# Multi-query attention with a parallel FFN on one core: the FFN's input weights load behind the q weights, the other weights behind the first q tile

## The chip, the core and the metric

One core of a Trainium2 chip runs the whole kernel in one launch. The metric is device microseconds of an execution. Before the change the median of six runs is 739.34 us (738.37 to 739.84).

TensorE (PE) multiplies, ScalarE (ACT) does exponentials and tanh, VectorE (DVE) and GpSimd (POOL) do elementwise work, and SyncE (SP) issues nearly all transfers. Each engine takes its instructions strictly in the order in which the program lists them, and waits on semaphores where data come from another engine or from a transfer.

## What is computed

```python
xn = _layernorm(x, axis=-1)                 # x: 1 x 2048 x 640
q = (xn @ wq)  # 32 heads of 20;  k = xn @ wk, v = xn @ wv: one head of 20 for all
scores = jnp.einsum("bhqd,bkd->bhqk", q, k) * (Dh ** -0.5)
p = _softmax(scores, axis=-1)
o = jnp.einsum("bhqk,bkd->bhqd", p, v)
A = o.transpose(0, 2, 1, 3).reshape(B, S, H * Dh) @ wo
B = silu(xn @ w1) @ w2                      # 640 -> 1728 -> 640
return x + A + B
```

All inputs and the output are bfloat16. There is one batch of 2048 rows.

## The kernel before

**Tiles and steps.** The 2048 rows are four chunks of 512 queries (QC) and 16 key tiles of 128 (KT). A unit is one head of one chunk, 128 in all; three units make a group, and a group takes 16 steps, one for each key tile. A step (`do_S`, L750) is up to three 128x512 score tiles, one for each unit, in three PSUM banks (L769). The 43 groups make 688 steps; the last group has two units. The exponential of a step is one ACT instruction over two or three tiles (L787). Where `want_dve` (L740) says so, the third tile goes to DVE instead: it is clipped into an integer that is read as a bfloat16 (L801), and two shifted copies of it, one from DVE (L869, up to three tiles at once) and one from POOL (L807), are added up with it by PE. PV (L857) are the products with v; a tile on DVE needs three or more of them. They come in four column groups of one bank, which DVE evacuates at the end of a group (L972), a transposing transfer turns (L931) and POOL normalizes (L939 to L958).

**The other work.** The FFN of a chunk is 14 first products of five matmuls (`h_job`, L1084), each with a tanh on ACT (L1092, into one of the two halves of `tb`) and a multiply on DVE (L1097), and then eight half tiles of 14 matmuls each (`out_job`, L1146; 448 in all). The output projection is L1151, 144 in all; in the last chunk some of it is held in PSUM (L1209, L1214). The q tiles of a chunk are `qd_job` (L1050): DVE evacuates one (L1057), and SP copies its heads to their rows in `qT` (L1066), five to eight transfers each. The first eight heads of chunk 0 come from two q jobs of their own (`q_job`, L1025).

**What sets the order.** Nothing is ordered by the hardware's timing: `Sched` plays the program through before it is built, with a guessed duration for each operation, and writes down one list for each engine. PE asks `step` (L565): a score row if it can run, else PV, else a matmul of the next job in `misc`, else a filler matmul on zeros (L687, L693, L706). Jobs of `misc` come strictly in turn and mostly share one PSUM bank (7). `fill_chunk` (L1227) puts a chunk's jobs in when its first score row comes, each with a step before which it may not begin (L1256 to L1265). On other engines the ready operation with the lowest priority number is next; an operation with `lock` set is planned apart from the locked ones of the other of DVE and POOL.

**The prologue.** `prologue` (L1284) loads x in 16 row tiles, takes means and variances (DVE L1411 and L1413, or ACT L1396 and L1399 for ACT_STATS), and an inverse root by two Newton rounds for each batch of BATCHES on the engine in NW_ENG (`newton`, L1440: nine small operations on DVE, twelve on POOL). It normalizes (`norm`, L1429, the engine in NORM_ENG: L1436 on POOL or DVE, L1431 on ACT) and transposes, on PE (`tr_job`, L1511, evacuated at L1522) or with a transfer for the tiles in DT (L1489). Keys (`k_job`, L1532, evacuated at L1540, shifted copy on POOL at L1542), values (L1556, L1565) and q jobs follow in the order of PRO. SP's list is: four x, a part of wq, twelve x, the rest of wq (L1321), the transposes as they come, two fills of the unused rows of `qT` from `tb` (L1500), w1 (L1503), wo (L1505), four x tiles again (L1222), w2 (L1326), then the q copies. w2 lies over the normalized x tiles and waits for their transposes. POOL doubles wo (L1547) behind the last key job.

Of the kernel before, what the change touches and what calls it, by code (L numbers as in the profile page):

```python
# [12 lines left out]
ALU = mybir.AluOpType  # L13

P = 128
D = 640
H = 32
DH = 20
DC = 5
# [5 lines left out]
QC = S // QW  # L25
KT = S // P
F = 1728
FC = 14
FLAST = F - 13 * P
HT = 8  # L30
# [15 lines left out]
NBLK = 31  # L46
NZ = 4
ZB = 3
Y_POOL = True
Y_TIME = 0.72  # L50
Y_LOCK = False
Y_SLOW = 0.1
H_FIRST = 4
NEARLY = 2
LASTPV = 16
DVE_LAST = 1
ZWAIT = 6
SWITCH = 0.105
S_LEAD = 0.56
PV_PRESS = 12  # L60
DVE_TH = 2.8
U_PRIO = 1.1
X_PRIO = 0.8
PACE = (0.9, 0.9, 0.9, 0.9)
# [4 lines left out]
OVER = 0.1  # L69
FLUSH_G = 0  # L70
NOD = 0
PV_HOLD = 9
Q_EVERY = 2
DT_ISSUE = 1.28
UT_ISSUE = 1.05
DT = (4, 5, 8, 9, 10, 11, 12, 13, 14, 15)
NORM_P = 0.5
DVE_FROM = 8
PRO = "t6 v0 k2 t7 k3 k4 q1 v1 v2 k5 k6 k7 v3 d0"
ACT_STATS = (4, 6, 9, 12, 14)  # L80
NW_ENG = ("dve", "pool", "dve", "pool")
NORM_ENG = ("pool", "pool", "pool", "pool", "dve", "act", "act", "dve", "act", "dve", "dve", "act")
BATCHES = ((0, 4), (4, 8), (8, 12), (12, 16))


class Op:
# [268 lines left out]
class Builder:  # L355
# [382 lines left out]


    def want_dve(self, t):  # L740
        if t < DVE_FROM or t % KT >= KT - NOD or t >= self.T - DVE_LAST:
            return False
        sc = self.sc
        back = sc.t["dve"] - sc.t["pe"]
        for op in sc.pend["dve"]:
            back += op.dur
        back += len(self.zblocks) * 0.6
        return back < DVE_TH

    def do_S(self, t, now):  # L750
        sc = self.sc
# [1 line left out]
        us = self.groups[g]  # L753
        nh = len(us)
        self.started = True
        for c in sorted(set(x // H for x in us)):
            if c not in self.filled:
                self.filled.add(c)
                self.fill_chunk(c, t)
        dv = self.want_dve(t)  # L760
# [282 lines left out]
    def qd_job(self, c, m, step=-1):  # L1043
        sc = self.sc
        lo, hi = (Q0 if c == 0 else QN)[m]
        rows = hi - lo
        mms = []
        for k in range(DC):
            def f(pe, b, k=k):
                return pe.matmul(self.bk(b, 0, QW, 0, rows), self.wq[:, k, lo:hi], self.xnT[:, k, c * QW:(c + 1) * QW],  # L1050
                                 start=(k == 0), stop=(k == DC - 1))
            mms.append((t_mm(QW), f))

        def consume(b):
            sl = self.nqd % 2
            self.nqd += 1
            sc.new("dve", t_dve_ps(QW), lambda v: v.tensor_scalar(self.qd[0:rows, sl, :], self.bk(b, 0, QW, 0, rows), C1,  # L1057
                                                                  None, ALU.mult), [("B", b)], [("qd", sl)],
                   prio=X_PRIO, name=f"qev{c}_{m}")
            sem = sc.sem(f"q{c}_{m}")  # L1060
            ops = []
            heads = range(lo // DH, -(-hi // DH))
            for h in heads:
                a, z = max(lo, h * DH), min(hi, h * DH + DH)
                r = (h % 4) * SLOT + a - h * DH
                ops.append(sc.dma("sp", lambda q, a=a, z=z, r=r, h=h: q.dma_start(  # L1066
                    self.qT[r:r + z - a, h // 4, c % 2, :], self.qd[a - lo:z - lo, sl, :]), [("qd", sl)],
                    [("qb", c % 2, h)], (z - a) * QW * 2, sem=sem, name="qdma"))
# [158 lines left out]
    def fill_chunk(self, c, t):  # L1227
# [56 lines left out]
    def prologue(self):  # L1284
# [19 lines left out]
        def load_w(eng, key, pieces, tag, nb, over=()):  # L1304
            deps = sc.deps_of((), [tag] + list(over))
# [13 lines left out]
        for n in range(4, NT):  # L1319
            load_x(n)  # L1320
        load_w("sp", "q", [lambda q, c=c: q.dma_start(self.wq[:, c, 80:], self.A_wq[c * P:(c + 1) * P, 80:])  # L1321
                           for c in range(DC)], ("wqd", 1), P * D * 2)
        w2p = []
        for fk in range(FC):
            rows = P if fk < FC - 1 else FLAST
            w2p.append(lambda q, fk=fk, rows=rows: q.dma_start(self.w2[0:rows, fk, :],  # L1326
                                                               self.B_w2[fk * P:fk * P + rows, :]))

        def load_w2():
            load_w("sp", "2", w2p, ("w2",), P * D * 2, [("xn", i) for i in range(14)] + [("idf",)])  # L1330
# [98 lines left out]
        def norm(n, eng, prio, ra):  # L1429
            if eng == "act":  # L1430
                np_("act", t_act(D) + 0.186, lambda v: v.activation(  # L1431
                    xa(n), self.xslot(n), AF.Identity, scale=self.rstd[:, n:n + 1],
                    bias=self.nb[:, n:n + 1]), self.xkeys(n) + [("nb", n), ("rs", ra)], [("xn", n)],
                    prio=prio, name=f"norm{n}")
                return
            np_(eng, 0.36 if eng == "dve" else 0.87, lambda v: v.tensor_scalar(  # L1436
                xa(n), self.xslot(n), self.rstd[:, n:n + 1], self.nb[:, n:n + 1], ALU.mult, ALU.add),
                self.xkeys(n) + [("nb", n), ("rs", ra)], [("xn", n)], prio=prio, name=f"norm{n}")

        def newton(a, b_, pr, eng):  # L1440
            v_ = self.tmp[:, 0, a:b_]
# [3 lines left out]

            def nw(fn, r, w):
                ch.append(np_(eng, 0.09 if eng == "dve" else 0.16, fn, r, w, prio=pr, name="nw"))
                if len(ch) > 1:
                    ch[-2].then = ch[-1]
            nw(lambda v: v.tensor_scalar(v_, self.mv[:, a:b_, 1], EPS, None, ALU.add), mvk(a, b_), [("va", a)])  # L1450
# [43 lines left out]
        pool(0.95, lambda g: g.tensor_scalar(self.tb[:, 0, :], self.zero[:, 0:QW], self.offq[:, :], 1.0, ALU.add, ALU.mult),  # L1494
             [("zero",), ("offq",)], [("tb", 0)])
        tb = self.tb[:, 0, :]
        for par in range(2):
            h0 = 2 if par == 0 else 0
            rep = bass.AP(self.tb, tb.offset, [list(tb.ap[0]), [0, HT - h0], list(tb.ap[1])])
            op = sc.dma("sp", lambda q, par=par, h0=h0, rep=rep: q.dma_start(self.qT[:, h0:HT, par, :], rep), [("tb", 0)],  # L1500
                        [("qb", par, h) for h in range(4 * h0, H)], P * (HT - h0) * QW * 2, sem=sem(f"qz{par}"))
            op.inc_no = 1
        load_w("sp", "1", [lambda q, c=c: q.dma_start(self.w1[:, c, :], self.B_w1[c * P:(c + 1) * P, :])  # L1503
                           for c in range(DC)], ("w1",), P * F * 2)
        load_w("sp", "o", [lambda q, c=c: q.dma_start(self.wo[:, c, :], self.A_wo[c * P:(c + 1) * P, :])  # L1505
                           for c in range(DC)], ("wo",), P * D * 2)
        def tr_job(n):
            mms = []
            for k in range(DC):
# [5 lines left out]
            def consume(b):  # L1515
                src = self.bk16(b)[:, 0:DC * P].rearrange("p (c t) -> p c t", c=DC)
                dst = self.xnT[:, :, n * P:(n + 1) * P]
                if n in (0, 2):
                    sc.new("act", t_act(D), lambda a: a.activation(dst, src, AF.Copy), [("B", b)], [("xnT", n)],
                           prio=2.0, name=f"xT{n}")  # L1520
                else:
                    sc.new("dve", 0.40, lambda v: v.tensor_copy(dst, src), [("B", b)], [("xnT", n)],  # L1522
                           prio=0.5 if n < 4 else 3.0, name=f"xT{n}")
                if n == max(i for i in range(13) if i not in DT):
                    load_w2()
            return Job(f"tr{n}", mms, xnk(n)[:1] + [("idb",)], consume)

        def k_job(j):
# [7 lines left out]
            def consume(b):  # L1536
# [4 lines left out]
                       name=f"kev{j}")  # L1541
                sc.new("pool", t_pool(256), lambda g: g.tensor_scalar(d1, dst, self.offk[:, :], 1.0, ALU.add,  # L1542
                                                                      ALU.mult), [("kT", j), ("offk",)],
                       [("kT1", j)], prio=1.0, name=f"k1_{j}")
                if j == KT // 2 - 1:
                    for c in range(DC):
                        pool(0.7, lambda g, c=c: g.tensor_scalar(self.wo[:, c, :], self.wo[:, c, :], 2.0, 1.0, ALU.mult,  # L1547
                                                                 ALU.mult), [("wo",)], [("wo",)], prio=2.0)
# [100 lines left out]
```

## Time and profile before

| | |
|---|---|
| median of six runs | 739.34 us |
| profiled execution, its own time | 739.32 us |
| its span, first to last instruction | 737.5 us |
| PE busy (matmuls, ends modelled) | 710.8 us, 96% |
| ACT busy | 691.4 us, 94%, of it L787 658.3 in 688 |
| DVE busy | 665.7 us, 90%, of it L801 432.8 in 646 |
| POOL busy | 538.3 us, 73% |
| mean granted PE clock | 0.991 |
| first, last score row | 16.7 us, 710.6 us |
| first tanh (L1092) | 64.86 us, behind 32 exponentials |
| w1 issued by SP | 39.5 to 44.9 us |
| w2 issued by SP | 49.7 to 56.4 us |

Times are from the start of the span. In a row of the timeline the first number is the start, the second the time to the end of the last of the merged instructions; the bracket is how long the engine was idle before, and who ended that. The duration of an instruction is longer than the distance to the next one, because they overlap at their ends: what counts in a full engine is the distance from start to start.

### The profile page before, as it was taken

How to read it: one execution, taken by the hardware profiler on the slowest of the kernel's cores; microseconds unless marked ns; L12 is line 12 of the kernel's file. 1: busy time of each engine (PE TensorE's matmuls, PEld its weight loads, DVE VectorE, ACT ScalarE, POOL GpSimd, SP SyncE). 2: the span in 40 equal slices, each digit the busy share in tenths (PEclk: the TensorE clock that was granted, in tenths of full speed). 3: DMA queues.
4: the chain of work that ended last, by engine and by line, in shares of the span. 5: the costliest groups of instructions: out<-in, count | busy, mean ns of one | idle time of the engine just before them, and what ended most of it. 6: DMA issues, size and time to landing. Idle time of an engine off the chain costs nothing.

```text
span 737.5 us, 18883 instructions
## 1 busy us (share of the span) xinstructions
PE 710.8 (96%) x6798; PEld 229.9 (31%) x6852; DVE 665.7 (90%) x1206; ACT 691.4 (94%) x780; POOL 538.3 (73%) x929
## 2 busy tenths in 40 slices
PE   9799999999999999999999999999999999999998
PEld 4422222233332223223333322222233332322245
DVE  7778998999999999989999999999999999989973
ACT  6878999999999999999999999999999999999940
POOL 5458777787787777777878877777787877777750
PEclk9879999999999999999999999999999999999999
DMA  6494010000002021100001101110002000200101
GB/s 191 79 324 126 18 24 17 21 17 16 9 16 44 17 58 40 34 8 9 9 8 27 34 16 43 52 31 16 8 9 44 10 8 16 80 9 8 31 16 36
DMA packets 58466, 29.14 MB, mean 40 GB/s; under 512 B 44390, under 2 KB 57734, under 8 KB 58374
## 3 DMA queue, kind: packets, MB, share of 16 engines
q1 hardware_dynamic: 56918, 27.71, 14.7%
q8 instruction: 56, 0.92, 0.5%
q10 hardware_dynamic: 1456, 0.22, 0.2%
q14 instruction: 36, 0.29, 0.1%
HBM read 11.36 MB, written 2.62 MB: 19 GB/s over the span
## 4 chain that ended last, share of the span: by engine, by line
PE 61%; ACT 19%; DVE 5%; issue 5%; POOL 0%; DVEq 0%; ACTq 0%; POOLq 0%
PE psall L857 21%; PE psall L769 20%; ACT sbt L787 17%; PE psall L1146 9%; PE psall L1084 5%; DVE sbt L801 3%; PE psall L1151 2%; PE psall L1050 2%; ACT sbt L1092 2%; DVE sbt L869 1%; PE psall L693 0%; DVE sbt L972 0%; DVE sbt L1057 0%; PE psall L1214 0%; DVE sbt L1097 0%
## 5 line engine op out<-in xcount | busy, mean ns | idle before, releaser
L787 ACT ACTIVATE sbt<-psall 128x1024 bf16<-128x1024 f32 (+2 forms) x688 | 658.3, 1090 | 15.3 <-PE psall L769 14.4
L807 POOL TENSOR_TENSOR sbt<-sbt 128x256 int32<-128x256 int32 x646 | 447.2, 698 | 150.8 <-DVE sbt L801 122.4
L801 DVE TENSOR_SCALAR sbt<-psall 128x512 int16<-128x512 f32 x646 | 432.8, 684 | 34.8 <-PE psall L769 27.4
L769 PE MATMUL psall<-sbt 32*128 32x512 bf16 x2048 | 270.1, 386 | 7.9 <-ACT sbt L787 4.4
L857 PE MATMUL psall<-sbt 128*32 128x512 bf16 x3524 | 270.4, 385 | 2.1 <-DVE sbt L869 0.7
L769 PEld LDWEIGHTS psall<-sbt 32*128 32x128 bf16 x2048 | 68.6, 91 | 252.8 <-issue 103.0
L869 DVE TENSOR_SCALAR sbt<-sbt 128x1536 int16<-128x1536 int16 (+2 forms) x230 | 134.6, 586 | 2.8
L857 PEld LDWEIGHTS psall<-sbt 128*32 128x32 bf16 x3524 | 67.7, 94 | 113.1 <-issue 76.1
L1146 PE MATMUL psall<-sbt 128*128 128x320 bf16 x448 | 86.2, 302 | 0.0
L1084 PE MATMUL psall<-sbt 128*128 128x512 bf16 (+1 forms) x242 | 75.5, 384 | 5.0 <-issue 3.5
L1146 PEld LDWEIGHTS psall<-sbt 128*128 128x128 bf16 x448 | 35.1, 97 | 43.4 <-issue 33.8
L1097 DVE SCALAR_TENSOR_TENSOR sbt<-sbt,psall 128x512 bf16<-128x512 bf16 (+1 forms) x56 | 38.1, 680 | 4.3 <-ACT sbt L1092 3.7
L1092 ACT ACTIVATE sbt<-psall 128x512 bf16<-128x512 f32 (+1 forms) x56 | 37.8, 675 | 0.0
L972 DVE CAST sbt<-psall 128x512 bf16<-128x512 f32 x43 | 29.3, 682 | 2.5 <-PE psall L857 2.4
L1084 PEld LDWEIGHTS psall<-sbt 128*128 128x128 bf16 (+1 forms) x280 | 18.8, 98 | 39.2 <-issue 28.2
L1050 PE MATMUL psall<-sbt 128*128 128x512 bf16 (+1 forms) x81 | 26.6, 385 | 2.7 <-issue 1.4
L1151 PE MATMUL psall<-sbt 128*128 128x320 bf16 x144 | 28.7, 303 | 0.4 <-DVE sbt L1181 0.4
L944 POOL TENSOR_TENSOR sbt<-sbt 128x44 f32<-128x44 f32 x84 | 25.2, 300 | 1.0
L958 POOL TENSOR_TENSOR sbt<-sbt 128x240 bf16<-128x240 f32 (+2 forms) x44 | 25.5, 579 | 0.6 <-DVE sbt L949 0.2
L706 PE MATMUL psall<-sbt 128*128 128x512 bf16 (+2 forms) x67 | 18.1, 418 | 4.5 <-DVE sbt L1565 3.0
L1178 ACT ACTIVATE sbt<-psall 128x320 bf16<-128x320 f32 x4 | 1.5, 438 | 20.7 <-PE psall L1151 20.7
L942 POOL CAST sbt<-sbt 128x168 f32<-128x168 bf16 x42 | 14.1, 336 | 7.6 <-DMA sbt<-sbt 7.5
(94 smaller groups left out, 222.2 us busy)
## 6 DMA issues: line engine op xcount, KB each, us to landing
sbt<-in_A_x_dram SPq DMA_DIRECT2D x32, 160.0 KB, 3.5
out_dram<-sbt SPq DMA_DIRECT2D x15, 160.0 KB, 1.9
sbt<-in_B_w_dram SPq DMA_DIRECT2D x5, 432.0 KB, 7.3
sbt<-sbt SPq DMA_DIRECT2D x105, 20.0 KB
sbt<-in_B_w_dram SPq DMA_DIRECT2D x13, 160.0 KB, 5.7
sbt<-sbt SPq DMA_TRANSPOSE x68, 2.4
sbt<-sbt SPq DMA_DIRECT2D x1, 1024.0 KB, 7.3
sbt<-in_A_wo_dram SPq DMA_DIRECT2D x5, 160.0 KB, 6.8
```

Of the source, the lines that this page charges most:

```text
L769: ins = pe.matmul(self.bk(par3 + j), self.kT[r:r + SLOT, kk, kt * P:(kt + 1) * P], self.qT[r:r + SLOT, h // 4, (x // H) % 2, :], start=Tru ...
L787: return a.activation(self.E[:, b0 * QW:(b0 + na) * QW], self.ps[:, par3 * BANK:(par3 + na) * BANK], AF.Exp, scale=ACT_SCALE)
L801: return v.tensor_scalar(self.Z[:, zs, zp * QW:(zp + 1) * QW], self.bk(bb), 0.0, ZMAX, ALU.max, ALU.min)
L807: sc.new("pool", Y_TIME, lambda v: v.tensor_tensor(self.Y[:, zs, 1, zp * QW:(zp + 1) * QW].bitcast(I32), self.Z[:, zs, zp * QW:(zp + 1) * ...
L857: return pe.matmul(self.bk(UBANK, 0, QW, q * SLOT, (q + 1) * SLOT), self.v[:, w, kt, :], x, start=start, stop=stop, tile_position=(0, q * ...
L869: sc.new("dve", Y_SLOW + t_dve_4x(w), lambda v, k=k: v.tensor_scalar(self.Y[:, zs, k, 0:n * QW], Z, float(PH[k + 1][0]), None, ALU.add), z ...
L1050: return pe.matmul(self.bk(b, 0, QW, 0, rows), self.wq[:, k, lo:hi], self.xnT[:, k, c * QW:(c + 1) * QW], start=(k == 0), stop=(k == DC - 1))
L1084: return pe.matmul(self.bk(b, 0, QW, 0, rows), self.w1[:, k, fk * P:fk * P + rows], self.xnT[:, k, c * QW:(c + 1) * QW], start=(k == 0), s ...
L1092: sc.new("act", t_act(QW), lambda a: a.activation(t, src, AF.Tanh, scale=0.5), [("B", b)], [("tb", tp)], prio=X_PRIO, name=f"th{c}_{fk}")
L1097: sc.new("dve", t_dve_ps(QW), lambda v: v.scalar_tensor_tensor(out=self.hT[0:rows, fk, :], in0=t, scalar=1.0, in1=src, op0=ALU.add, op1=AL ...
L1146: return pe.matmul(self.bk(b, 0, 320), self.hT[0:rows, fk, i * P:(i + 1) * P], self.w2[0:rows, fk, e0:e0 + 320], start=(m == 0), stop=(m = ...
L1151: return pe.matmul(self.bk(b, 0, 320), self.oT[:, k, i * P:(i + 1) * P], self.wo[:, k, e0:e0 + 320], start=(m == 0 and src != "ps"), stop= ...
```

## The change

It has six parts.

1. w1 goes to SP right behind the rest of wq, ahead of the transposes.
2. w2, wo, the doubling of wo and the second fill of `qT` wait for the first q tile's evacuation (`late_loads`, called by `qd_job(0, 0)`); w2 used to be queued behind a transpose job, wo ahead of it.
3. A chunk's jobs are put in `misc` AHEAD = 30 steps before its first score row, with due steps as much earlier; in chunk 0 they may begin at step H0_STEP = 10 (16 before).
4. The inverse roots are taken in three batches of 4, 6 and 6 tiles, all on DVE; norms are shared out anew (ACT 6, POOL 5, DVE 5, the first four included); NORM_P is their priority; norms, Newton operations and the shifted key copies are locked between DVE and POOL.
5. The prologue's jobs stand in another order, with the q tile d0 behind v2 instead of last.
6. Constants of the planner: the share of DVE tiles (DVE_TH), the pressure at which PV goes first, the hold before the first PV, the first FFN jobs ahead of the projection, and when q jobs are mixed in (Q_FROM).

```diff
+AHEAD = 30
+Q_FROM = 8
+H0_STEP = 10
+KT_ACT = ()
-H_FIRST = 4
+H_FIRST = 8
-PV_PRESS = 12
-DVE_TH = 2.8
+PV_PRESS = 8
+DVE_TH = 2.6
-PV_HOLD = 9
+PV_HOLD = 11
-DT = (4, 5, 8, 9, 10, 11, 12, 13, 14, 15)
-NORM_P = 0.5
+DT = (4, 5, 6, 9, 10, 11, 12, 13, 14, 15)
+NORM_P = 4.5
-PRO = "t6 v0 k2 t7 k3 k4 q1 v1 v2 k5 k6 k7 v3 d0"
+PRO = "v0 t7 t8 v1 k2 k3 k4 q1 v2 d0 k5 k6 k7 v3"
-NW_ENG = ("dve", "pool", "dve", "pool")
-NORM_ENG = ("pool", "pool", "pool", "pool", "dve", "act", "act", "dve", "act", "dve", "dve", "act")
-BATCHES = ((0, 4), (4, 8), (8, 12), (12, 16))
+NW_ENG = ("dve", "dve", "dve")
+NORM_ENG = ("pool", "pool", "pool", "pool", "act", "pool", "act", "act", "dve", "act", "act", "act")
+BATCHES = ((0, 4), (4, 10), (10, 16))
...
-        for c in sorted(set(x // H for x in us)):
-            if c not in self.filled:
+        for c in range(QC):
+            if c not in self.filled and t >= self.first_step[c] - AHEAD:
...
+            if c == 0 and m == 0:
+                self.late_loads(("qd", sl))
...
-            if qs and n % Q_EVERY == Q_EVERY - 1:
+            if qs and n >= (Q_FROM if c else 0) and n % Q_EVERY == Q_EVERY - 1:
...
+        s0 -= AHEAD
+        s1 -= AHEAD
         if c == 0:
-            s0 += KT
+            s0 = H0_STEP
...
+        load_w("sp", "1", [lambda q, c=c: q.dma_start(self.w1[:, c, :], self.B_w1[c * P:(c + 1) * P, :])
+                           for c in range(DC)], ("w1",), P * F * 2)
...
-        for par in range(2):
+        def qz(par, extra=()):
...
+        qz(0)
+
+        def late_loads(key):
+            load_w2([key])
+            load_w("sp", "o", [lambda q, c=c: q.dma_start(self.wo[:, c, :], self.A_wo[c * P:(c + 1) * P, :])
+                               for c in range(DC)], ("wo",), P * D * 2, (), [key])
+            for c in range(DC):
+                pool(0.7, lambda g, c=c: g.tensor_scalar(self.wo[:, c, :], self.wo[:, c, :], 2.0, 1.0, ALU.mult, ALU.mult),
+                     [("wo",)], [("wo",)], prio=2.0)
+            qz(1, [key])
+        self.late_loads = late_loads
```

KT_ACT is empty and changes nothing. The norms', Newton's and key copies' `.lock = True`, and the lines that loaded w1, wo and w2 at their old places, are left out above.

More of the change, by code (lines that the diff above doesn't have):

```diff
@@ L740, in want_dve @@
     def want_dve(self, t):
-        if t < DVE_FROM or t % KT >= KT - NOD or t >= self.T - DVE_LAST:
+        if t < DVE_FROM or t % KT >= KT - NOD or t >= self.T - DVE_LAST or t % KT in KT_ACT:
             return False
@@ L1302, in load_x, with load_w @@
             op.inc_no = 1
-        def load_w(eng, key, pieces, tag, nb, over=()):
-            deps = sc.deps_of((), [tag] + list(over))
+        def load_w(eng, key, pieces, tag, nb, over=(), extra=()):
+            deps = sc.deps_of(extra, [tag] + list(over))
             for f in pieces:
@@ L1327, in prologue, with load_w2 @@
                                                                self.B_w2[fk * P:fk * P + rows, :]))
-        def load_w2():
-            load_w("sp", "2", w2p, ("w2",), P * D * 2, [("xn", i) for i in range(14)] + [("idf",)])
+        def load_w2(extra):
+            load_w("sp", "2", w2p, ("w2",), P * D * 2, [("xn", i) for i in range(14)] + [("idf",)], extra)
         np_ = sc.new
@@ L1437, in norm @@
                 xa(n), self.xslot(n), self.rstd[:, n:n + 1], self.nb[:, n:n + 1], ALU.mult, ALU.add),
-                self.xkeys(n) + [("nb", n), ("rs", ra)], [("xn", n)], prio=prio, name=f"norm{n}")
+                self.xkeys(n) + [("nb", n), ("rs", ra)], [("xn", n)], prio=prio, name=f"norm{n}").lock = True
         def newton(a, b_, pr, eng):
@@ L1447, in nw @@
                 ch.append(np_(eng, 0.09 if eng == "dve" else 0.16, fn, r, w, prio=pr, name="nw"))
+                ch[-1].lock = True
                 if len(ch) > 1:
@@ L1496, in prologue @@
         tb = self.tb[:, 0, :]
-        for par in range(2):
+        def qz(par, extra=()):
             h0 = 2 if par == 0 else 0
             rep = bass.AP(self.tb, tb.offset, [list(tb.ap[0]), [0, HT - h0], list(tb.ap[1])])
-            op = sc.dma("sp", lambda q, par=par, h0=h0, rep=rep: q.dma_start(self.qT[:, h0:HT, par, :], rep), [("tb", 0)],
+            op = sc.dma("sp", lambda q: q.dma_start(self.qT[:, h0:HT, par, :], rep), [("tb", 0)] + list(extra),
                         [("qb", par, h) for h in range(4 * h0, H)], P * (HT - h0) * QW * 2, sem=sem(f"qz{par}"))
             op.inc_no = 1
[L1503 to L1506, printed above, removed]
+        qz(0)
[8 more added lines that the diff above has]
+        self.late_loads = late_loads
         def tr_job(n):
@@ L1523, in consume @@
                            prio=0.5 if n < 4 else 3.0, name=f"xT{n}")
-                if n == max(i for i in range(13) if i not in DT):
-                    load_w2()
             return Job(f"tr{n}", mms, xnk(n)[:1] + [("idb",)], consume)
@@ L1543, in consume @@
                                                                       ALU.mult), [("kT", j), ("offk",)],
[L1544 to L1548, printed above, removed]
+                       [("kT1", j)], prio=1.0, name=f"k1_{j}").lock = True
             return Job(f"kv{j}", mms, [("xnT", 2 * j), ("xnT", 2 * j + 1), ("wk",), ("ost", 2, 0), ("ost", 2, 1)], consume)
```

## The prediction

> **What bounds the kernel now.** I read the page first, then the busy time by stage, then ScalarE's (ACT) and TensorE's (PE) instructions in order of time, then the waits.
>
> ```profile
> span 737.5 us, 18883 instructions
> ...
> ACT  6878999999999999999999999999999999999940
> ...
> PEclk9879999999999999999999999999999999999999
> ```
>
> ACT is full from the fifth slice to the last but two. It loses time at the start and at the end, and the granted PE clock dips only at the start. By stage (columns: PE, PEld, DVE, ACT, POOL busy us, then clock, DMA share, GB/s):
>
> ```profile
> 17.18:38.86 21.68, 17.48 (x152) 8.73 (x152) 16.24 (x52) 17.96 (x19) 11.21 (x29) 0.86 0.44 78
> 38.86:86.30 47.44, 44.28 (x406) 12.82 (x411) 39.05 (x71) 40.14 (x44) 34.26 (x56) 0.92 0.54 176
> 86.30:700.00 613.70, 599.64 (x5901) 183.77 (x5950) 577.41 (x996) 612.53 (x678) 472.76 (x789) 1.00 0.11 24
> 710.60:737.50 26.90, 23.46 (x180) 13.98 (x179) 10.01 (x25) 2.64 (x6) 1.83 (x3) 1.00 0.07 26
> ```
>
> A "step" is one row of score matmuls (L769) and its exponential (L787); there are 688. Step 8 starts its exponential at 38.86, step 50 at 86.3, and the last score row is at 710.6. So there are three regimes: a start with holes in ACT, 614 us in which ACT idles 1.2 us, and a tail of 26.9 us in which ACT does 2.64 us and PE works alone. The tail, PE by time:
>
> ```profile
> 711.96 1.90 PE L857 MATMUL psall<-sbt 128*32 128x512 bf16 x25
> 713.80 1.33 PE L1146 MATMUL psall<-sbt 128*128 128x320 bf16 x7
> 716.74 10.61 PE L1146 MATMUL psall<-sbt 128*128 128x320 bf16 x70
> 727.29 2.35 PE L1151 MATMUL psall<-sbt 128*128 128x320 bf16 x16
> 732.73 1.33 PE L1151 MATMUL psall<-sbt 128*128 128x320 bf16 x8
> ```
>
> L1146 is the FFN's second product. 10.61/70 = 0.152 us each, back to back: this backlog is the end of the kernel. Then ACT in order of time, with its idle time in brackets, and SP's issues:
>
> ```profile
> 29.55 1.45 ACT L787 ACTIVATE sbt<-psall 128x1536 bf16<-128x1536 f32 x1 [2.50 <-PE psall L769]
> 30.90 1.72 ACT L1431 ACTIVATE sbt<-sbt 128x640 bf16<-128x640 bf16 x2
> 38.86 1.02 ACT L787 ACTIVATE sbt<-psall 128x1024 bf16<-128x1024 f32 x1 [0.39 <-PE psall L769]
> 47.07 4.90 ACT L787 ACTIVATE sbt<-psall 128x1024 bf16<-128x1024 f32 x5 [2.84 <-PE psall L769]
> 67.84 1.94 ACT L787 ACTIVATE sbt<-psall 128x1024 bf16<-128x1024 f32 x2 [2.34 <-PE psall L769]
> 505.56 3.92 ACT L787 ACTIVATE sbt<-psall 128x1024 bf16<-128x1024 f32 x4
> 509.18 0.79 ACT L1092 ACTIVATE sbt<-psall 128x512 bf16<-128x512 f32 x1
> ```
>
> ```profile
> 49.70 6.70 SPq L1326 DMA_DIRECT2D sbt<-in_B_w_dram  x14
> 59.10 5.78 SPq L1066 DMA_DIRECT2D sbt<-sbt  x7
> ```
>
> Three large holes. At 29.55 PE waited for key and value evacuations behind a slow DVE. At 47.07 the last key job (its POOL copy is at 45.99) held the score row. At 67.84 step 32 is the first that needs heads 8 and on, whose seven q copies were issued only at 59.1 to 64.9, behind w2's fourteen pieces. ACT's pitch when full is (509.18 − 505.56)/4 = 0.905 us for two tiles; a third tile makes it about 1.35 (29.55 to 30.90), so 0.43 us a tile.
>
> **What the Trainium skill says.** "SBUF — State Buffer", Who interferes with whom: VectorE and GpSimd share one port pair under an exclusive lock, so tiny ops can be blocked for a neighbour's whole instruction. The trace agrees:
>
> ```profile
> 7.33 0.20 DVE L1451 TENSOR_SCALAR sbt<-sbt 128x4 int32<-128x4 int32 x1
> ...
> 19.92 0.83 DVE L1451 TENSOR_SCALAR sbt<-sbt 128x4 int32<-128x4 int32 x1
> ```
>
> The second ran beside POOL's norm (L1436). "TensorE: Matmul & The Clock Gate", What's actually happening: an idle window halves PE's clock; the trace has a clock of 0.86 before 38.86, where PE is idle 4.2 of 21.7 us. "DMA: Bandwidth & Descriptors", Queues, rings and completion order: SP's transfers are taken in ring order on each DMA engine, and a semaphore lands only after earlier writes. The trace agrees: x lands 3.5 us after issue (median), w1 and wo in the crowd at 39 to 47 us after 7.3 and 6.8.
>
> **The change part by part.** How instructions move I take from the order of the built programs, which holds no times; all durations are from the trace.
>
> *Tail.* After the last score row the old order has 89 L1146 matmuls, the new one 10: FFN chunks are opened AHEAD = 30 steps earlier. 79 × 0.152 = 12.0. The ten that stay still cover the waits for the last evacuation and its PE transposes (716.5, 5.9 after the last row). Check from the other end: 5.9, transposes 0.2, 8 matmuls of L1151 1.2, the 24 of L1209 and L1214 3.3 (729.34 to 732.60), 8 more 1.3, and 3.4 from PE's end to the span's end make 15.3 against 26.9. I take **−11.7**.
>
> *ACT's work.* The new order has 626 tiles on DVE instead of 646, so 20 tiles move to ACT: 20 × 0.43 = 8.6. Two more norms on ACT: 2 × 0.86 = 1.7 (row at 30.90). By place: before step 50 four tiles and two norms, less one tanh (0.48) that comes later, +2.9. From step 50 on 16 tiles and that tanh, **+7.3**; ACT has no idle time there to hide it. Relieved are DVE (20 × 0.68 of L801, some 17 us in all) and POOL (20 × 0.70), which bound nothing there.
>
> *PE's work in that phase.* It takes up the 79 matmuls (12.0) and 1.3 us of FFN and q matmuls that came before step 50, and loses some 37 PV matmuls at about 0.054 (12 take 0.22 more than 8), so about +11. The room is in the score rows' waits:
>
> ```profile
> PEld psall L769 <- ACT sbt L787: 63.2, 164, 0.7
> PEld psall L769 <- DVE sbt L801: 45.1, 112, 0.8
> ```
>
> Each begins 0.23 us after the row before anyhow (the "issue" rows), so the true waits are 63.2 − 164 × 0.23 = 25 and 45.1 − 112 × 0.23 = 19: 44 us. ACT's +7.3 widens it. Bounds of the extra cost: −4 (S no longer waits for DVE as often) to +4 (all 11 that isn't under ACT's 7.3). I take **+1.2**.
>
> *The start.* The gaps of ACT between 17.18 and step 50 are 0.82, 2.50, 0.39, 0.39, 0.51, 0.37, 2.84, 0.42, 0.31, 2.34: 10.9. In the new order: (a) both later inverse-root batches run on DVE, six tiles each, locked against POOL's norms; nine ops at about 0.2 make 2.0 us (7.12 to 9.13) instead of 4.1 (19.36 to 23.5), so norms 10 to 15 can start near 26.4 where ACT, after norm 8, two exponentials and the q weight copy, is free at 25.4: about 1.0 for 0.82. (b) Exponential 4 stands behind five norms, so the 2.50 is filled with work. (c) The holes of 0.3 to 0.5 lie under PE's half clock; I let all six (2.4) stay. (d) The last key job stands behind 11 score rows, not 14; 0.5 stays. (e) The first q tile (d0) moves ahead of the last keys: evacuated near 37, its copies leave behind the transposes (36.1), one fill and four x loads (2.6) and eight w2 pieces (3.8), by 43 to 48. Step 8 now comes near 37 (ACT free at 30.8 behind the norms, four wide exponentials at 1.35, some gap), step 32 at 37 + 24 × 0.905 + 2 × 0.43 + 1.5, near 61, so 2.34 goes. Left 3.9 of 10.9: −7.0, with +2.9 above **−4.1**. Bounds: −7.5 and +2.9.
>
> *What is moved in SP's queue.* w1 goes out at 11.2 to 16.5, where SP idles until 19.89; its data (2.2 MB at the 350 GB/s seen at 40 to 50 us, an estimate of 6.3) end about when the first transpose starts, so 0, at worst 1. w2, wo and the second fill go behind the first q evacuation: 14 pieces (6.7), seven copies (5.8), wo (2.5), fill: SP is through near 54 to 56. Two waits hang on this. The scaling of wo stands in POOL before about the 22nd third-tile add (L807): wo lands near 60, POOL is there near 60; behind it are those adds, and PE's PV rows behind them. And the first tanh writes tb, which the second fill reads: so although the first FFN matmuls stand at steps 18 and 19, the tanh stands behind 36 exponentials, near 66, and the fill lands at 59 to 63. I cost both at 0, with up to 3 us above. **FFN jobs don't really begin early**: at step 100 the new order has 55 first-product matmuls against 60. The gain in order comes over the next 500 steps.
>
> Sum: 737.5 − 11.7 + 7.3 + 1.2 − 4.1 = 730.2. The profiled execution took 739.32 with this span, 1.8 around it, and is at the median (739.34): **732.0**.
>
> **Rivals.** *Holes stay* (the start isn't filled as the order intends): +2.9 in place of −4.1, 739.0. For it: the wait near 67 only moves to other late loads. Against: the three big holes each lose their cause. *PE adds up with ACT*, the slower one: from step 50 on both are over 97% busy, and each score row waits for the later of PE and ACT; if waits no longer overlap, PE's 11.3 come on top of ACT's 7.3: 732.0 + 10.1 = 742.1. It decides as soon as it costs over 8.5 of those 11.3. For it: L1146 blocks of three or four must fit between score rows. Against: 44 us of waits, and ACT alone is late on almost every row. *DVE's relief counts*: −4 for +1.2, and the start at its best, −7.5: 732.0 − 5.2 − 3.4 = 723.4; at half of both 727.7.
>
> **How the numbers follow.** Forecast (728 to 737) 0.65; DVE's relief (723 to 728) 0.10; holes stay (737 to 740.5) 0.12; PE adds up (740.5 to 745) 0.13. The range 726 to 740 leaves out the slower case and about half of the better one. 0.2%, about what a measurement of this kernel can tell from no change, is 1.5 us: faster is below 737.9 (all of the first two, a sixth of the third, 0.77), same 0.10, slower 0.13.
>
> **What would show it.** PE after the last score row: ten L1146, about 15 us to the end; if it is 27 the order isn't what I read. ACT from step 50 to the last exponential: longer by 8.5; 15 or more is the slower rival. Step 50 at about 82 (before 86.3), no idle time over 1.5 before it. If ACT idles before its first tanh, or POOL before the wo scaling, the late loads bite.

## The result, and the profile after

The changed kernel takes 737.23 us in the median of 18 runs (735.45 to 739.49), the kernel before 739.51 in 37. The ratio is 0.9965 with an interval of 0.9957 to 0.9973: 0.3% faster, where 1.0% was forecast. The sign was right, the time is inside the range, and about two thirds of the gain is missing. The profiled execution took 737.44 us, with a span of 735.6.

From the page of the changed kernel, the span, ScalarE's (ACT's) busy tenths and the granted clock of TensorE (PE):

```profile
span 735.6 us, 18666 instructions
...
ACT  6996999999999999999999999999999999999972
...
PEclk9998999999999999999999999999999999999999
```

From the fifth slice on ACT is full up to the last two, which are a 7 and a 2 in place of 4 and 0. But its fourth slice (55 to 74 us) is only a 6, and the PE clock dips in that same slice. Busy time by stage, columns as before:

```profile
38.36:85.77 47.41, 41.23 (x399) 12.16 (x402) 34.84 (x63) 40.86 (x43) 31.75 (x52) 0.93 0.42 125
85.77:700.00 614.23, 599.69 (x5820) 187.11 (x5866) 560.54 (x961) 612.23 (x670) 451.55 (x759) 1.00 0.10 23
720.24:735.60 15.36, 11.29 (x98) 6.72 (x96) 7.34 (x18) 2.56 (x5) 2.58 (x4) 0.95 0.13 43
```

The last row is the tail from the last score row on: 15.4 us in place of 26.9. The first row is where the gain is missing: ACT is busy 40.86 of 47.41 us. PE at the start of the tail shows the ten matmuls of the FFN's second product that are left (L1152 here, L1146 before):

```profile
720.56 2.12 PE L861 MATMUL psall<-sbt 128*32 128x512 bf16 x28
722.62 1.12 PE L1152 MATMUL psall<-sbt 128*128 128x320 bf16 x7
...
723.69 0.67 PE L1152 MATMUL psall<-sbt 128*128 128x320 bf16 x3
```

ACT's rows with idle time ahead of them, up to step 50:

```profile
26.70 4.17 ACT L1441 ACTIVATE sbt<-sbt 128x640 bf16<-128x640 bf16 x5 [0.49 <-DVE sbt L1479]
...
39.88 22.47 ACT L791 ACTIVATE sbt<-psall 128x1024 bf16<-128x1024 f32 x23 [0.50 <-PE psall L861]
...
66.17 1.02 ACT L791 ACTIVATE sbt<-psall 128x1024 bf16<-128x1024 f32 x1 [3.81 <-PE psall L773]
...
68.63 1.02 ACT L791 ACTIVATE sbt<-psall 128x1024 bf16<-128x1024 f32 x1 [1.44 <-PE psall L773]
...
71.71 3.28 ACT L791 ACTIVATE sbt<-psall 128x1536 bf16<-128x1536 f32 x3 [0.55 <-PE psall L773]
```

The three large holes of before (2.50, 2.84, 2.34) are gone: after 39.88 ACT runs 23 exponentials without a gap. In their place a new hole of 3.81 + 1.44 + 0.55 = 5.80 us stands at steps 34 to 37. A score row (L773) is named as what ended it each time, so the question is what held that row. PE, then GpSimd (POOL), then the issues on SP, each in order of time:

```profile
60.35 0.39 PE L773 MATMUL psall<-sbt 32*128 32x512 bf16 x3
...
64.39 0.40 PE L861 MATMUL psall<-sbt 128*32 128x512 bf16 x4 [3.64 <-POOL sbt L811]
...
65.51 0.61 PE L773 MATMUL psall<-sbt 32*128 32x512 bf16 x3 [0.65 <-DVE sbt L805]
```

```profile
55.34 0.92 POOL L811 TENSOR_TENSOR sbt<-sbt 128x256 int32<-128x256 int32 x1 [0.55 <-DVE sbt L805]
62.34 0.33 POOL L946 CAST sbt<-sbt 128x168 f32<-128x168 bf16 x1 [6.08 <-DMA sbt<-sbt]
```

```profile
52.78 2.48 SPq L1519 DMA_DIRECT2D sbt<-in_A_wo_dram  x5
55.30 0.69 SPq L1512 DMA_DIRECT2D sbt<-sbt  x1
56.03 2.18 SPq L935 DMA_TRANSPOSE sbt<-sbt  x1
```

Read from the bottom. SP issues the transpose of group 0's U (L935) at 56.03, right behind wo and the second fill of qT (L1512, 1 MB). It lands 6.2 us after its issue; the median of the 42 transposes of this kind in the same profile is 2.4. POOL waits 6.08 us for it at L946, the first operation of group 0's normalisation. POOL's third-tile adds (L811) are queued behind, a PV row (L861) waits for one of those for 3.64 us, and the score row is queued behind the PV row on PE. The row that then comes takes 0.61 us in place of 0.39: PE has been idle, and the granted clock in the trace is 0.50 from 65.2 to 72.0. That is the larger part of the 1.44, but not of the 0.55: in the first kernel below, whose clock stays at 1.00, ACT waits 0.59 and 0.49 at the same two steps. The fall of the clock agrees with the Trainium skill, "TensorE: Matmul & The Clock Gate", What's actually happening, which says that a window of idleness halves the clock.

The trace of the kernel before already had this wait, only shorter. There the transpose (L931) goes out behind w2, lands after 5.0 us, and POOL waits 1.62 for it:

```profile
57.76 1.23 SPq L931 DMA_TRANSPOSE sbt<-sbt  x1
62.77 0.33 POOL L942 CAST sbt<-sbt 128x168 f32<-128x168 bf16 x1 [1.62 <-DMA sbt<-sbt]
```

### The profile page after: what moved, and what is told of

The parts are those of the page before. It is cut to its first block, busy times and chain, and to the rows that moved or that the text cites. A ratio compares the mean times of both kernels' runs of the same rounds, so it can differ in the third digit from the quotient of the medians.

```text
span 735.6 us, 18666 instructions
## 1 busy us (share of the span) xinstructions
PE 705.3 (96%) x6746; PEld 229.0 (31%) x6798; DVE 649.9 (88%) x1180; ACT 701.3 (95%) x782; POOL 517.1 (70%) x886
## 4 chain that ended last, share of the span: by engine, by line
PE 72%; ACT 13%; DVE 9%; issue 5%; DMA 0%; POOL 0%; DVEq 0%; ACTq 0%; POOLq 0%
PE psall L861 24%; PE psall L773 23%; ACT sbt L791 11%; PE psall L1152 10%; PE psall L1090 7%; DVE sbt L805 4%; PE psall L1157 2%; PE psall L1054 2%; PE psall L710 2%; ACT sbt L1098 1%; DVE sbt L873 1%; DVE sbt L976 1%; PE psall L697 1%; ACT sbt L1441 1%; DMA sbt<-sbt 0%
## 5 line engine op out<-in xcount | busy, mean ns | idle before, releaser
L791 ACT ACTIVATE sbt<-psall 128x1024 bf16<-128x1024 f32 (+2 forms) x688 | 666.4, 1105 | 14.1 <-PE psall L773 12.3
L811 POOL TENSOR_TENSOR sbt<-sbt 128x256 int32<-128x256 int32 x626 | 429.4, 693 | 172.7 <-DVE sbt L805 124.0
L805 DVE TENSOR_SCALAR sbt<-psall 128x512 int16<-128x512 f32 x626 | 419.1, 684 | 47.2 <-PE psall L773 39.1
L773 PE MATMUL psall<-sbt 32*128 32x512 bf16 x2048 | 269.9, 385 | 12.1 <-ACT sbt L791 6.6
L861 PE MATMUL psall<-sbt 128*32 128x512 bf16 x3470 | 263.2, 384 | 4.3 <-POOL sbt L811 3.6
L773 PEld LDWEIGHTS psall<-sbt 32*128 32x128 bf16 x2048 | 69.4, 91 | 252.0 <-ACT sbt L791 86.8
L873 DVE TENSOR_SCALAR sbt<-sbt 128x1536 int16<-128x1536 int16 (+1 forms) x218 | 129.9, 597 | 3.2
L861 PEld LDWEIGHTS psall<-sbt 128*32 128x32 bf16 x3470 | 66.0, 94 | 112.4 <-issue 70.0
L1152 PE MATMUL psall<-sbt 128*128 128x320 bf16 x448 | 87.7, 303 | 0.0
L1152 PEld LDWEIGHTS psall<-sbt 128*128 128x128 bf16 x448 | 33.4, 97 | 44.7 <-issue 35.1
L946 POOL CAST sbt<-sbt 128x168 f32<-128x168 bf16 x42 | 14.0, 333 | 11.2 <-DMA sbt<-sbt 11.0
L710 PE MATMUL psall<-sbt 128*128 128x512 bf16 (+3 forms) x71 | 19.1, 421 | 2.2 <-POOL sbt L1351 1.5
L1157 PEld LDWEIGHTS psall<-sbt 128*128 128x128 bf16 x144 | 11.5, 97 | 15.0 <-issue 10.4
```

What stands on the lines that cost most here:

```text
L773: ins = pe.matmul(self.bk(par3 + j), self.kT[r:r + SLOT, kk, kt * P:(kt + 1) * P], self.qT[r:r + SLOT, h // 4, (x // H) % 2, :], start=Tru ...
L791: return a.activation(self.E[:, b0 * QW:(b0 + na) * QW], self.ps[:, par3 * BANK:(par3 + na) * BANK], AF.Exp, scale=ACT_SCALE)
L805: return v.tensor_scalar(self.Z[:, zs, zp * QW:(zp + 1) * QW], self.bk(bb), 0.0, ZMAX, ALU.max, ALU.min)
L811: sc.new("pool", Y_TIME, lambda v: v.tensor_tensor(self.Y[:, zs, 1, zp * QW:(zp + 1) * QW].bitcast(I32), self.Z[:, zs, zp * QW:(zp + 1) * ...
L861: return pe.matmul(self.bk(UBANK, 0, QW, q * SLOT, (q + 1) * SLOT), self.v[:, w, kt, :], x, start=start, stop=stop, tile_position=(0, q * ...
L873: sc.new("dve", Y_SLOW + t_dve_4x(w), lambda v, k=k: v.tensor_scalar(self.Y[:, zs, k, 0:n * QW], Z, float(PH[k + 1][0]), None, ALU.add), z ...
```

## The experiments

Theory A is the chain just read: the transpose behind the fill. Theory B is that the hole belongs to POOL's order, or to the crowd of loads as such. The first four kernels differ from the changed one in SP's order alone, rearranged after the plan is made; every other engine's order is the same to the instruction.

**The transpose ahead of the fill.**

```diff
+        sp = b.sc.order["sp"]
+        fill = next(o for o in sp if o.mode == P * HT * QW * 2)
+        sp.remove(fill)
+        sp.insert(1 + [o.name for o in sp].index("uTd"), fill)
         lists = b.sc.emit()
```

> The changed kernel with one place in SP's queue altered: the transpose of group 0's U (L935) is issued ahead of the 1 MB second fill of qT (L1512) in place of behind it. All other queues are the same. Theory A (the transpose lands 6.2 us after its issue because the fill lies ahead of it in the DMA rings; GpSimd (POOL) waits 6.1 us for it, PE's PV rows wait for POOL's third-tile adds, ScalarE (ACT) idles 3.8 and then 1.4 and 0.55 more under the halved PE clock): it lands within 4 us of its issue near 55.3, POOL waits at most 3, ACT's hole near 66 shrinks from 5.8 us to under 1.5, and the kernel takes 731.5 to 733.5 us against 737.2 of the changed kernel. Theory B (the hole belongs to the order of POOL's work, or to wo, w2 and the copies in the crowd, and the transpose is only what is named): the hole stays at 5 to 6 us somewhere between 60 and 75, and the time within 1 of 737.2.

Measured: 732.89 us (ratio to before 0.9902, 0.9889 to 0.9915). The transpose lands 3.7 us after its issue, POOL's wait is 3.0 us, the hole 0.52 + 0.59, and a 0.49 further on. Theory B is out: POOL's order and the loads are the same, and the hole is nearly gone.

**The second fill back behind the first.**

```diff
+        sp.remove(fill)
+        first = next(o for o in sp if o.mode == P * (HT - 2) * QW * 2)
+        fill.deps = set(first.deps)
+        sp.insert(1 + sp.index(first), fill)
```

> The changed kernel with the second fill of qT (L1512) put back right behind the first one in SP's queue (as in the kernel before), all other queues the same. Theory A: the transpose of group 0's U now lies behind wo's pieces only, lands about 3 us after its issue near 55, ACT's hole near 66 goes and the time is 731.5 to 733.5. Theory B (the crowd as such): the 1 MB is only moved ahead of the x tiles, w2 and the q copies, which come 3 to 5 us later; the hole stays or moves ahead to step 32's wait for its copies, 736 to 740.

Measured: 736.92 us (0.9957, 0.9943 to 0.9970). The expectation of theory A missed, and the time lies in the range that theory B gave for this kernel. The transpose does land sooner after its issue, 3.6 us, but it is issued later: behind the two fills SP needs 5.12 us for the four x loads where it needed 2.93, and the transpose goes out 39.5 us after the first exponential instead of 38.0. POOL waits 4.8, and the hole is 2.37 + 1.62 = 4.0. It still ends with this transpose, so the chain holds; but the megabyte costs time in both places ahead of the transpose, here through its issue and there through its landing.

**The transpose ahead of wo and the fill.** (`ut` is moved, with `sp.insert(sp.index(fill) - DC, ut)`.)

> The changed kernel with the transpose of group 0's U (L935) issued ahead of wo's five pieces and of the second fill in SP's queue, all other queues the same. Theory A: issued near 52.8, it lands near 55.5 before POOL asks for it, so POOL's wait of 6.1 us at L946 goes altogether; the time is at or up to 1 us below that of the kernel with the transpose ahead of the fill alone, 731 to 733. wo comes about 1.2 us later and its scaling at 65 has room for that. Theory B: within 1 of 737.2; and if wo's landing was what counted, the scaling (L1522) now waits and the time is 738 or more.

Measured: 731.27 us (0.9882, 0.9869 to 0.9895), the fastest of the study: 0.8% below the changed kernel and 1.2% below the kernel before. In its trace, SP, POOL and ACT:

```profile
52.42 1.24 SPq L935 DMA_TRANSPOSE sbt<-sbt  x1
```

```profile
56.28 0.92 POOL L811 TENSOR_TENSOR sbt<-sbt 128x256 int32<-128x256 int32 x1 [0.55 <-DVE sbt L805]
57.15 0.32 POOL L946 CAST sbt<-sbt 128x168 f32<-128x168 bf16 x1
```

```profile
42.66 22.47 ACT L791 ACTIVATE sbt<-psall 128x1024 bf16<-128x1024 f32 x23 [0.92 <-PE psall L773]
```

POOL takes L946 without a wait, and ACT has no gap between 42.66 and 75.96.

**w1 late again.** (Its five pieces behind the first fill.)

> The changed kernel with w1's five pieces (L1331) issued right behind the first fill of qT, near 37 us, as in the kernel before, in place of behind the q weights at 11.2; all other queues the same. This undoes the part of the change that loads w1 early. If w1 early costs the start something (first exponential at 18.07 in the changed kernel, 17.18 before), the first exponential comes 0.9 earlier, near 17.2; if that shift is from run to run, it stays between 17.2 and 18.1 without a tie to this edit. Theory A: SP was busy without a break from 36.5 to 57.2, so all that stands behind, the q copies, w2, wo, the fill and group 0's transpose, comes 3.4 us later (five issues at 0.7) and lies behind 2.2 MB more: the hole near 66 grows by 3 to 6 us, or step 32 waits for its copies too, 740 to 744. Theory B: the hole keeps its size, 736 to 738.

Measured: 740.80 us (1.0010, 1.0002 to 1.0019). Its waits between 55 and 75 us (in total, times, longest):

```profile
POOL sbt L946 <- DMA sbt<-sbt: 9.3, 1, 9.3
ACT sbt L791 <- PE psall L773: 8.5, 2, 7.0
```

So one chain in five doses:

| order on SP | POOL waits at L946, us | ACT's hole, us | median, us |
|---|---|---|---|
| transpose ahead of wo and fill | 0 | 0 | 731.27 |
| transpose ahead of fill | 3.0 | 1.1 | 732.89 |
| fill early | 4.8 | 4.0 | 736.92 |
| as changed | 6.1 | 5.8 | 737.23 |
| w1 late | 9.3 | 8.5 | 740.80 |

Some 2 us of the wait are covered in the second row, 0.3 to 0.8 in the others. What is left, ACT's hole, goes to the end time at 1.0 to 1.5 us for each us, measured from the first row. Loading w1 early is worth 3.6 us in this order of SP, and not because FFN matmuls start sooner: PE's order is the same. With w1 late the transpose goes out 39.9 us after the first exponential instead of 38.0, and lands after 7.6 us instead of 6.2. The first comes of w1's five issues. The second stays open: w1's last piece had landed at 46.2, 12 us before this transpose was issued.

The next four start from the 731.27 kernel and ask which part of the change shortens the tail, and what that costs. The order of the built program already says what does not: with AHEAD at 0, with H0_STEP at 16, with both, or with PV_HOLD at 9, the changed kernel is the same on all five engines, instruction for instruction; so is the kernel before with AHEAD = 30 put in. The FFN jobs are a first-in, first-out list with a standing backlog, so an earlier opening finds nothing free. What moves most of the backlog is PV_PRESS and DVE_TH.

```diff
-PV_PRESS = 8
+PV_PRESS = 12
```

> The kernel with group 0's transpose ahead of wo and the fill (731.3 us), with PV_PRESS put back from 8 to 12, DVE_TH left at 2.6. In the order of the built program 52 matmuls of the FFN's second product (L1152) stand after the last score row in place of 10, and 2 tiles more go to VectorE (DVE). Theory A (the prediction's sum: a matmul left for the tail costs 0.152 us there, in the phase before it lies almost all in waits; a tile that goes to ScalarE costs 0.43): +42 x 0.152 - 2 x 0.43 = +5.5, 736.8 us, with the time from the last exponential to the end 6.4 longer and the time from step 50 to the last exponential shorter by 1 to 2. Theory C (PE adds up: a matmul costs the same in both places): the stretch from step 50 shortens by 6 or 7 too, 730.4 us.

Measured: 735.05 us (0.9941, 0.9926 to 0.9956). From the last exponential to the end it takes 20.67 us, 5.8 more than the kernel it starts from; step 50 to the last exponential takes 634.6, 0.5 less. In these two stretches that is theory A. In the profile the start, from the first exponential to step 50, was 3.2 shorter. I do not explain that fully: PE's order differs a little early on, but two profiles with one and the same order up to step 50 (this series' start and Q_FROM, below) also differ by 2.1 there, 63.7 and 61.6. So differences of 2 to 3 us in the start of single profiles carry no weight here.

```diff
-DVE_TH = 2.6
+DVE_TH = 2.8
```

> The kernel with group 0's transpose ahead of wo and the fill (731.3 us), with DVE_TH put back from 2.6 to 2.8, PV_PRESS left at 8. In the order of the built program 15 tiles go back from ScalarE to VectorE, and 65 matmuls of the FFN's second product stand after the last score row in place of 10. Theory A (the prediction's sum): 55 x 0.152 - 15 x 0.43 - 9 PV matmuls fewer in the tail x 0.054 = +1.4, 732.7 us: the tail 8 longer, the stretch from step 50 to the last exponential 6 to 8 shorter. Theory C (PE adds up): only the tiles count, 724.8 us, the stretch from step 50 shorter by 14.

Measured: 734.24 us (0.9931, 0.9913 to 0.9950). The tail is 7.3 longer, as expected. But the stretch from step 50 is only 1.35 shorter: the work that ACT gives back there is 4.6 us (tiles at the pitches of full work), and 3.3 of it returned as other waits. Neither theory had that. The start took 3.9 less, of which 2 to 3 may be chance.

> The kernel with group 0's transpose ahead of wo and the fill (731.3 us), with both DVE_TH (2.8) and PV_PRESS (12) put back as in the kernel before. In the order of the built program 19 tiles go back to VectorE, 112 matmuls of the second product and 6 of the first stand after the last score row in place of 10. Theory A: 102 x 0.152 + 6 x 0.22 + 7 x 0.054 - 19 x 0.43 = +9.0, 740.3 us, a tail of 32 from the last exponential. Theory C: 723.1 us. A third reading, that the steps loaded early and opened early (AHEAD, H0_STEP, both left as in the changed kernel) shorten the tail by themselves: the tail stays at 15.

Measured: 738.76 us (0.9987, 0.9977 to 0.9997), with 33.24 us from the last exponential to the end and 626.1 from step 50. Theory A in kind, 1.5 below its number. With both constants back, the better start (59.2 us from the first exponential to step 50, 69.1 before) is nearly all given back in the tail, which is 7.1 longer than before. Part of that is work that PE no longer does in the holes of the start: 11 of the FFN's first-product matmuls stand before step 50 in place of 16, an estimated 1 us at 0.22 each. What makes the rest is not shown.

> The kernel with group 0's transpose ahead of wo and the fill (731.3 us), with DVE_TH put back to 2.8 and PV_PRESS lowered to 4. In the order of the built program no matmul of the second product stands after the last score row, and 18 tiles go back to VectorE: the short tail without the work given to ScalarE. Theory A: -18 x 0.43 = -7.7, and 0 to -1.5 for the ten matmuls: 722 to 723.6 us; the stretch from step 50 to the last exponential back near 627. A rival, D: PV is now held back until 27 of the 31 slots of E are in use, so on the chip exponentials wait for a slot that PE's PV frees, and the stretch from step 50 stays at 635 or grows, 731 or more.

Measured: 737.56 us (0.9976, 0.9965 to 0.9987). The tail is short (12.6) and the tiles are on DVE, but the stretch from step 50 takes 645.9. Theory D in kind. ACT waits 15.0 us for score rows there (25 waits), where the kernel with DVE_TH 2.8 alone has 7.9. One of them, in order of time:

```profile
374.22 1.48 PE L861 MATMUL psall<-sbt 128*32 128x512 bf16 x21
...
375.63 0.39 PE L773 MATMUL psall<-sbt 32*128 32x512 bf16 x3
...
376.13 1.02 ACT L791 ACTIVATE sbt<-psall 128x1024 bf16<-128x1024 f32 x1 [1.29 <-PE psall L773]
```

PV rows that were held back run in a block of 21 matmuls, and the score row stands behind it. The mechanism differs from the one expected in one point: ACT waits for the row, not for a slot of E.

Three more looked for a better version between these.

> The kernel with group 0's transpose ahead of wo and the fill (731.3 us), with DVE_TH at 2.7, between the changed kernel's 2.6 and the 2.8 of before; PV_PRESS stays 8. In the order of the built program 12 tiles go back to VectorE, and 23 matmuls of the second product stand after the last score row in place of 10. Theory A (the prediction's prices, 0.43 us a tile, 0.152 a matmul in the tail): 13 x 0.152 - 9 x 0.054 - 12 x 0.43 = -3.7, 727.6 us. What DVE_TH at 2.8 showed (the tiles' gain less 3.3 us of other waits between step 50 and the last exponential, so 0.2 us a tile net) gives 731.3 + 2.0 - 0.5 - 2.6 = 730.2.

Measured: 733.14 us (0.9905, 0.9892 to 0.9919). Both numbers missed: ACT's work from step 50 is 3.8 less, but the stretch is 1.7 longer; the last 38 steps alone are 2.8 longer. Giving tiles back to DVE is not worth 0.43 us each in this order.

> The kernel with group 0's transpose ahead of wo and the fill (731.3 us), with Q_FROM put back to 0, so that the q tiles of later chunks are spread from the start of each chunk as before. In the order of the built program the tiles on VectorE stay at 626 and none of the ten matmuls of the second product is left after the last score row. Theory A: these ten only cover waits there (the prediction's count of the tail from the other end), so 0 to -1.5: 729.8 to 731.3 us. The other reading, that Q_FROM is what spreads PE's work so that score rows come in time: the stretch from step 50 to the last exponential grows, 733 or more.

Measured: 731.39 us (0.9882, 0.9868 to 0.9895), the same as without the edit, so Q_FROM does nothing for the time here. But the parts have moved, and each reading is right in part: in the profiles the tail is 2.1 shorter (12.8 for 14.9), so the ten matmuls did not lie in waits alone, and the stretch from step 50 is 2.7 longer.

> The kernel with group 0's transpose ahead of wo and the fill (731.3 us), with DVE_TH 2.65 and PV_PRESS 7. In the order of the built program 6 tiles go back to VectorE and no matmul of the second product stands after the last score row. Theory A: -6 x 0.43, and 0 to -1.5: 727.2 to 728.7 us. Theory D, as PV_PRESS 4 showed (PV rows held back and then run in blocks of up to 21 matmuls, 1.5 us, ahead of a score row that ScalarE waits for): one step further on PV_PRESS costs some of the 15 us that four steps cost, so the stretch from step 50 to the last exponential is at 635 or more, and the kernel at 731 to 735.

Measured: 738.28 us (0.9980, 0.9971 to 0.9989). Theory D in kind, and dearer than it said: the stretch from step 50 takes 643.9.

Last, the two constants alone in the kernel before:

> The kernel before with two constants of the change alone, DVE_TH 2.6 in place of 2.8 and PV_PRESS 8 in place of 12; no load is moved, and the FFN chunks open where they did. In the order of the built program no matmul of the second product stands after the last score row (89 before), and 22 tiles more go to ScalarE. Theory A (the tail is shortened by these two constants, not by the loads and the earlier opening): the tail from the last exponential falls from 26.1 to 13, the stretch from step 50 grows by 9 to 12 (22 x 0.43 = 9.5, and up to 2.5 for other waits as in the changed kernel), the holes of the start stay at about 10: 739.4 - 13.3 + 9.5 + 2.5 = 738.1 us. A rival (PE adds up, as with PV_PRESS 7): score rows wait for PV blocks, the stretch grows by 18 or more, 743 us.

Measured: 748.50 us (1.0123, 1.0103 to 1.0144). The tail falls from 26.14 to 13.00 as theory A has it, so these two constants alone shorten it. The stretch from step 50 grows by 14.0, 2 above the range. And the start, which I took as unchanged, falls apart: ACT stands idle before FFN evacuations for 8.29 and 4.84 us and then 3.27 before step 32. The same transpose (L931 here, waited for at L942) is in the chain of the first, behind w2 this time:

```profile
64.46 0.33 POOL L942 CAST sbt<-sbt 128x168 f32<-128x168 bf16 x1 [5.05 <-DMA sbt<-sbt]
...
70.40 0.60 ACT L1092 ACTIVATE sbt<-psall 128x512 bf16<-128x512 f32 x1 [8.29 <-PE psall L1084]
```

The constants shorten the tail in either loading order. They cost 9 us with the old one and gain 7.5 with the new one and the transpose first (738.76 against 731.27). The 4.84 and the 3.27 come while PE works through 27 filler matmuls (L706, 70.16 to 79.34) that the plan had put there, so they belong to the planned order. That the place of the q copies and of this transpose behind w2 makes the difference is my reading of the trace; no run separates the two.

## Why the prediction was wrong, point by point

Spans of the profiled executions, before, changed, and with the transpose first (us):

| | forecast | changed | transpose ahead of wo and fill |
|---|---|---|---|
| first exponential | 0 | +0.9 | −0.4 |
| first exponential to step 50 | −4.1 | −1.4 | −5.4 |
| step 50 to last exponential | +8.5 | +9.85 | +10.1 |
| last exponential to the end | −11.7 | −11.2 | −11.25 |
| sum | −7.3 | −1.9 | −7.0 |

- **The step that failed is "What is moved in SP's queue".** It said "Two waits hang on this", the scaling of wo and the first tanh, and "I cost both at 0, with up to 3 us above". Both were indeed 0: POOL has no wait before its first scaling (65.10) and ACT none before its first tanh (69.55). A third wait hung on it and was not named: group 0's U transpose is itself an issue of SP, behind all the loads that the change moved. It cost 5.8 us of ACT's time, though the trace of before had POOL waiting 1.62 us for it. The last column shows that this step carries the miss: with the transpose first, the median is 731.27 against the 732.0 forecast. That it comes so near is luck in part, because two other errors offset each other: the start gained 1.3 more than forecast and the stretch from step 50 cost 1.6 more. The profile in that column is the slowest of its kernel's four executions.
- **The start.** The three large holes went, and step 32 came at 59.95 (near 61 forecast). For the first two the causes named fit the traces; no run takes back the new order of the prologue or of the inverse roots alone, so what each is worth isn't shown. The cause of the third was misread. It was put to the q copies standing behind w2's pieces, but w2's issues ended at 56.40, and the copies went out at 59.10, right behind the evacuation of their q tile:

```profile
58.25 0.68 DVE L1057 TENSOR_SCALAR sbt<-psall 128x512 bf16<-128x512 f32 x1
59.10 5.78 SPq L1066 DMA_DIRECT2D sbt<-sbt  x7
```

  So by the traces it is the earlier q tile (d0) that removed this hole: after the change it is evacuated at 35.2. No run moves it alone. Beside the new hole the gaps are 1.6 us where 3.9 was left; in the kernel with the transpose first they sum to 3.5. A slip in the text, without weight in the sum: the exponential at 38.86 before is step 10, step 8 was at 36.52.
- **The first exponential, 0.9 later.** Not a cost of the change: up to there the order, but for w1's place in one of them, is the same in the changed kernel and the eleven that start from it, and yet the time lies between 16.55 and 18.19 in their profiles. With w1 late it is 18.19, so w1 is not its cause. What sets it from run to run stays open.
- **The tail: right number, wrong cause.** Ten matmuls are left and 15.4 us, as forecast. But "FFN chunks are opened AHEAD = 30 steps earlier" is not why: AHEAD alters no instruction. DVE_TH and PV_PRESS did it.
- **From step 50 on.** ACT's extra work is +7.3, as forecast. The excess over it was put at +1.2 and is +2.5, half of it in the last 38 steps.
- **Rivals.** The result is nearest to *Holes stay* (739.0), and its "for it" line named the kind: "the wait near 67 only moves to other late loads". I gave that 0.12 and looked for the place at wo and the tanh. *PE adds up with ACT* did not happen at these constants. At PV_PRESS 7 and 4 the stretch from step 50 is 8.8 and 10.8 longer than in the kernel they start from; at 4 the trace shows another mechanism, PV rows in blocks.

## What to carry to other kernels

When loads are moved later in a queue, list every later issue of that queue, small ones included, and ask of each who waits for it and what is queued behind the waiter. Look for a short wait on such an issue in the trace of before. Here an issue that lands 2.4 us after going out in most groups landed after 6.2, and three engines stood behind it. Where a job list has a backlog, opening it earlier does nothing; look in the built order for the setting that changes how fast it drains, and price what that setting gives to the busiest engine.

## What the runs showed of the hardware

- A transpose of one U tile landed 2.4 us after issue in the median. Group 0's landed after 3.6 and 3.7 behind wo's pieces, 5.0 behind w2 (before), and 6.2 right behind a 1 MB fill on the same queue; there the fill landed at 61.5 and the transpose 0.8 later. The Trainium skill, "DMA: Bandwidth & Descriptors", Queues, rings and completion order, says that each DMA engine takes a queue's descriptors in the order of its ring; this agrees with it.
- What stands right ahead can slow the issuing side as well. Right behind both fills (1.75 MB) the four x loads took SP 5.12 us to issue, right behind one (0.75 MB) 2.9 to 3.7. It isn't the bytes ahead in all: with w1's 2.2 MB between that fill and the loads they took 1.89.
- PE was idle for 3.6 us and then ran score rows at 0.61 us in place of 0.39 until 72.0. An outage of 2.4 us in the kernel with the fill early was followed by rows of 0.44, 0.61 and then 0.39 again at 67.6. A hole costs more than its length: ACT's first wait of 2.37, 3.81 and 7.03 us became 3.99, 5.80 and 8.48 with those that followed, so the addition is 1.4 to 2.0 us and doesn't grow with the hole.
